# Attention with the keys on the partitions: PV in sixteen narrow matmuls, the output (not P) transposed by DMA, no row maximum, MLP last

## The chip, the cores and the metric

One core of one Trainium2 chip. The metric is the device time of one execution in microseconds (us), the median of several runs. "TensorE" is PE in the profile, "VectorE" DVE, "ScalarE" ACT. PSUM is the memory that matmuls write to, in banks; to *evict* a bank is to copy its content out, or to add it to an accumulator. PV is the product of the softmax's output P with V.

## The reference, cut to what matters

A block with adaptive layer norms: attention, then an MLP with ReLU, both on a sequence of 2048 rows of 512. Attention has 32 query heads that share 8 key/value heads of dimension 128, and looks at the last 512 keys.

```python
h = layernorm(x) * (1 + ca) + sa                 # sa, ca, ga, sb, cb, gb come from silu(c) @ w_mod
q = (h @ wq).reshape(1, 2048, 32, 128)           # wq 512 x 4096
p = softmax(q @ k.T * 128**-0.5)                 # k, v: the last W = 512 cached rows
x = x + ga * ((p @ v).reshape(1, 2048, 4096) @ wo)
h = layernorm(x) * (1 + cb) + sb
x = x + gb * (relu(h @ w1) @ w2)                 # w1 512 x 1792, w2 1792 x 512
```

## The kernel before

The rows are cut into 4 blocks of 512; a *unit* is one block and one head, 128 units in all. The loop takes one *step* per unit and records operations for each engine: `kb.op(stream, fn, reads, writes)` appends to that engine's own queue and works out the semaphores to wait for. So the order of the calls is the order in each engine's queue.

```python
def rec_qk(i, tl):          # scores, query rows on partitions: one 128x512 tile
    matmul(ps[sbk], lhsT=qT[:, 128 rows], rhs=kT[:, g, :])
    DVE  tensor_reduce(nm, ps[sbk], max, negate=True)                      # L865
    ACT  activation(P, ps[sbk], Exp, bias=nm, accum_out=lsum)              # L867

def rec_rn(i):              # normalise P, then transpose it
    DVE  reciprocal(rinv, lsum)
    POOL tensor_scalar(P, P, rinv, mult)       # x4                        # L885
    dma_start_transpose(PT, P)                 # 512 KB

def rec_pv(i, kc):          # 4 matmuls of 512 columns, V stationary       # L899
    matmul(ps[ob], lhsT=v[:, g, kc, :], rhs=PT[:, kc, :], start=(kc == 0), stop=(kc == 3))
    if kc == 3: DVE tensor_copy(oT[slot], ps[ob])                          # L914

# [...] output projection, one group of 16 matmuls per 128 rows, one PSUM bank
        def f(h, tl, t, ii):
            matmul(ps[wb], lhsT=oT[slot][:, rows], rhs=wo_sb[:, h, :], start=(ii == 0), stop=(ii == HQ - 1))  # L931
            if ii == HQ - 1:
                DVE tensor_copy / tensor_tensor(acc, ps[wb], acc, add)     # eviction, L936 / L938
            return ii == HQ - 1

def pop_wo(n, paced=False):             # one projection matmul per call ...
    if paced:
        if wo_state["skip"] > 0:        # ... but after a group has ended, one call is skipped,
            wo_state["skip"] -= 1       # so that the bank can be evicted; made up for later
            wo_state["debt"] += n
            return
        # [...]
```

The eviction is recorded in the same call as the group's last matmul. MLP matmuls (L1036, L1060) follow attention; the last projections overlap with them.

## Time and profile before

| | before |
|---|---|
| time, median | 628.3 us (627.1 to 632.0) |
| span of the profiled run | 626.4 us |
| first Q matmul | 17.8 us |
| attention, per unit | 3.67 us |
| last matmul to the end | 3.5 us |

The head of the page, with each engine's busy time:

```profile
span 626.4 us, 8650 instructions
PE 570.4 (91%) x2668; PEld 245.1 (39%) x2721; DVE 507.0 (81%) x1036; ACT 459.5 (73%) x1211; POOL 418.0 (67%) x607
```

From the list of costliest groups (line, engine, operation, output<-input, shapes, count | busy us, mean ns | idle before):

```profile
L885 POOL TENSOR_SCALAR arena<-arena 128x512 bf16<-128x512 bf16 x512 | 344.9, 692 | 88.9 <-DVE arena L878 88.5
L867 ACT ACTIVATE arena<-ps,arena 128x512 bf16<-128x512 f32 x512 | 348.0, 687 | 52.1 <-DVE arena L865 47.8
L865 DVE TENSOR_REDUCE arena<-ps 128x1 f32<-128x512 f32 x512 | 336.4, 680 | 18.1 <-PE ps L863 15.4
L899 PE MATMUL ps<-arena 128*128 128x512 bf16 x498 | 188.8, 380 | 8.8 <-DMA arena<-arena 8.4
...
L914 DVE CAST arena<-ps 128x512 bf16<-128x512 f32 x128 | 87.0, 680 | 9.5 <-PE ps L899 9.5
```

A matmul's record of 380 ns is not what it costs. In the timeline of TensorE (start, duration, what) the starts show it:

```profile
202.16 0.38 PE L899 MATMUL ps<-arena 128*128 128x512 bf16 x1
202.37 0.38 PE L931 MATMUL ps<-arena 128*128 128x512 bf16 x1
202.59 0.38 PE L863 MATMUL ps<-arena 128*128 128x512 bf16 x1
...
558.03 0.61 PE L592 MATMUL ps<-arena 128*128 128x128 bf16 x8
```

Matmuls of 512 columns start 0.2157 us apart. The last line is 8 transposes of 128 columns, each with its own weight load: 0.61 us less one record of 0.219 us, over 7, is 56 ns from start to start.

So a unit's 16 matmuls (4 each for Q, scores, PV, projection) need 3.45 us, 128 units 442 us, and the MLP's 448 need 97 us: 538 of the 626 us. TensorE bounds the kernel; the other 88 us are the start, the end, and waits in attention. In mid-attention VectorE is 97% busy. The waits (engine and line <- releaser: us in total, times, longest):

```profile
PEld ps L863 <- ACT arena L867: 69.2, 133, 1.2
PE ps L863 <- ACT arena L867: 15.8, 40, 0.7
PEld ps L931 <- DVE arena L936: 3.0, 5, 1.1
PEld ps L931 <- DVE arena L938: 2.5, 3, 0.8
```

Scores wait for the exp to free their bank. The projection hardly waits for its eviction.

### The profile page before, as it was taken

The page shows a single profiled execution, that of the slowest core. Times are in us where ns is not written, and L with a number is a line of the kernel's source. Part 1 is how long each engine was busy: PE and PEld are TensorE (multiplying, and loading weights), DVE is VectorE, ACT ScalarE, POOL GpSimd, SP SyncE. Part 2 cuts the span into 40 slices and gives each one's busy share as a digit, 9 for nine tenths or more (in the row PEclk, how much of TensorE's full clock was granted, in tenths as well). Part 3 has the DMA queues.
Part 4 walks back from the last instruction along what each step waited for, and adds up shares of the span by engine and source line. Part 5 has one row for each costly group of instructions (what it writes and reads, how often), then busy time and mean ns, then how long its engine had stood idle before and what let it go on. Part 6 is the DMA issues. An engine that isn't in the chain of part 4 may idle for free.

```text
span 626.4 us, 8650 instructions
## 1 busy us (share of the span) xinstructions
PE 570.4 (91%) x2668; PEld 245.1 (39%) x2721; DVE 507.0 (81%) x1036; ACT 459.5 (73%) x1211; POOL 418.0 (67%) x607
## 2 busy tenths in 40 slices
PE   2788789999899999999999999999989889989997
PEld 2222224344343344444434444434434334434443
DVE  4799899999899999999999999999999722362223
ACT  1799989799897888999989799989779633304310
POOL 3477769677797896778989867889969701702000
PEclk9999999999999999999999999999999989999999
DMA  9999998999997678787876878977787980000001
GB/s 234 207 225 198 219 210 155 200 211 215 196 219 134 123 123 153 142 154 149 152 146 115 159 130 148 159 137 135 135 135 131 184 224 1 1 33 1 33 26 42
DMA packets 292749, 89.17 MB, mean 142 GB/s; under 512 B 276064, under 2 KB 291680, under 8 KB 292704
## 3 DMA queue, kind: packets, MB, share of 16 engines
q1 hardware_dynamic: 292704, 88.63, 72.0%
q8 instruction: 21, 0.34, 0.2%
q14 instruction: 24, 0.20, 0.1%
HBM read 18.35 MB, written 2.10 MB: 33 GB/s over the span
## 4 chain that ended last, share of the span: by engine, by line
PE 52%; DVE 22%; DMA 11%; POOL 7%; ACT 6%; issue 2%; SPq 0%
DVE arena L865 12%; PE ps L931 11%; DMA arena<-arena 9%; PE ps L899 9%; PE ps L863 9%; PE ps L838 8%; PE ps L1060 8%; PE ps L1036 7%; ACT arena L867 5%; POOL arena L885 4%; DVE arena L599 3%; DVE arena L914 3%; DVE arena L562 2%; DMA arena<-in_B_w_dram 1%; ACT arena L847 1%
## 5 line engine op out<-in xcount | busy, mean ns | idle before, releaser
L885 POOL TENSOR_SCALAR arena<-arena 128x512 bf16<-128x512 bf16 x512 | 344.9, 692 | 88.9 <-DVE arena L878 88.5
L867 ACT ACTIVATE arena<-ps,arena 128x512 bf16<-128x512 f32 x512 | 348.0, 687 | 52.1 <-DVE arena L865 47.8
L865 DVE TENSOR_REDUCE arena<-ps 128x1 f32<-128x512 f32 x512 | 336.4, 680 | 18.1 <-PE ps L863 15.4
L863 PE MATMUL ps<-arena 128*128 128x512 bf16 x498 | 190.1, 382 | 18.9 <-ACT arena L867 15.8
L899 PE MATMUL ps<-arena 128*128 128x512 bf16 x498 | 188.8, 380 | 8.8 <-DMA arena<-arena 8.4
L838 PE MATMUL ps<-arena 128*128 128x512 bf16 x503 | 189.6, 379 | 2.2 <-DVE arena L599 0.8
L931 PE MATMUL ps<-arena 128*128 128x512 bf16 x504 | 177.4, 380 | 2.7 <-DVE arena L938 1.0
L867 ACT ACTIVATION_READ_ACCUMULATOR arena<-ps,arena 128x1 f32 x512 | 102.4, 200 | 0.0
L914 DVE CAST arena<-ps 128x512 bf16<-128x512 f32 x128 | 87.0, 680 | 9.5 <-PE ps L899 9.5
L863 PEld LDWEIGHTS ps<-arena 128*128 128x128 bf16 x512 | 49.6, 97 | 113.1 <-ACT arena L867 69.2
L847 ACT ACTIVATE arena<-ps 128x512 bf16<-128x512 f32 x128 | 76.0, 594 | 16.1 <-PE ps L838 16.1
L1049 ACT ACTIVATE arena<-ps 128x512 bf16<-128x512 f32 x56 | 33.4, 597 | 69.6 <-PE ps L1036 69.6
L899 PEld LDWEIGHTS ps<-arena 128*128 128x128 bf16 x512 | 50.1, 98 | 76.5 <-DMA arena<-arena 14.8
L931 PEld LDWEIGHTS ps<-arena 128*128 128x128 bf16 x512 | 49.6, 98 | 62.7 <-DVE arena L936 3.0
L838 PEld LDWEIGHTS ps<-arena 128*128 128x128 bf16 x512 | 50.1, 98 | 45.0 <-issue 0.8
L1036 PE MATMUL ps<-arena 128*128 128x512 bf16 x220 | 52.8, 384 | 6.5 <-DVE arena L599 2.8
L599 DVE TENSOR_SCALAR arena<-ps,arena 128x128 bf16<-128x128 bf16 x128 | 34.5, 333 | 24.0 <-PE ps L592 23.6
L1060 PE MATMUL ps<-arena 128*128 128x512 bf16 x220 | 48.8, 379 | 0.2
L1065 DVE TENSOR_TENSOR arena<-ps,arena 128x512 bf16<-128x512 f32 x16 | 11.1, 691 | 39.8 <-PE ps L1060 39.8
L943 POOL TENSOR_TENSOR arena<-arena 128x512 f32<-128x512 f32 x16 | 20.3, 1267 | 32.4 <-DVE arena L938 31.0
L1036 PEld LDWEIGHTS ps<-arena 128*128 128x128 bf16 x224 | 21.6, 98 | 32.5 <-DMA arena<-in_B_w_dram 4.4
L1060 PEld LDWEIGHTS ps<-arena 128*128 128x128 bf16 x224 | 21.8, 98 | 26.0
(40 smaller groups left out, 174.6 us busy)
## 6 DMA issues: line engine op xcount, KB each, us to landing
arena<-in_A_wq_dram SPq DMA_DIRECT2D x8, 512.0 KB, 5.4
arena<-in_A_wo_dram SPq DMA_DIRECT2D x8, 512.0 KB, 4.9
arena<-in_w_mod_dram SPq DMA_DIRECT2D x6, 512.0 KB, 5.6
arena<-in_A_x_dram SPq DMA_DIRECT2D x4, 512.0 KB, 5.3
arena<-arena SPq DMA_TRANSPOSE x128, 4.3
out_dram<-arena SPq DMA_DIRECT2D x16, 128.0 KB, 1.8
arena<-in_B_w_dram SPq DMA_DIRECT2D x1, 1792.0 KB, 8.0
arena<-in_B_w_dram SPq DMA_DIRECT2D x1, 1280.0 KB, 7.4
```

The source lines that it names most:

```text
L599: kb.op(DVE, lambda e, cc=cc: e.tensor_scalar(hnT[:, cc, ht * P:(ht + 1) * P], psb[bk][:, cc * P:(cc + 1) * P], sc_f(cc), sh_f(cc), op0=AL ...
L838: kb.op(PE, lambda e: e.matmul(ps[qb][:, :QB], wq_sb[:, k, h * Dh:(h + 1) * Dh], hnT[:, k, hn_cols(b)], start=(k == 0), stop=(k == DC - 1) ...
L847: kb.op(ACT, lambda e: e.activation(qT[qs], ps[qb][:, :QB], ACTF.Copy, scale=scale), reads=[R_ps[qb]], writes=[R_qT[qs]])
L863: kb.op(PE, lambda e: e.matmul(ps[sbk][:, :W], qT[qs][:, tl * P:(tl + 1) * P], kT_sb[:, g, :], start=True, stop=True), reads=[R_qT[qs], R_ ...
L865: kb.op(DVE, lambda e: e.tensor_reduce(nm[:, si:si + 1], ps[sbk][:, :W], axis=AX.X, op=ALU.max, negate=True), reads=[R_ps[sbk]], writes=[R ...
L867: kb.op(ACT, lambda e: e.activation(Pv[:, :, tl, :], ps[sbk][:, :W].rearrange("p (k q) -> p k q", k=KC), ACTF.Exp, bias=nm[:, si:si + 1], ...
L885: kb.op(POOL, lambda e, tl=tl, si=si: e.tensor_scalar(Pv[:, :, tl, :], Pv[:, :, tl, :], rinv[:, si:si + 1], 0.0, op0=ALU.mult, op1=ALU.add ...
L899: kb.op(PE, lambda e: e.matmul(ps[ob][:, :QB], v_sb[:, g, kc, :], PTv[:, kc, :], start=(kc == 0), stop=(kc == KC - 1)), reads=[R_v[g][kc], ...
L914: kb.op(DVE, lambda e: e.tensor_copy(oT[os_], ps[ob][:, :QB]), reads=[R_ps[ob]], writes=[R_oT[os_]], pre=pre)
L931: kb.op(PE, lambda e: e.matmul(ps[wb][:, :D], oT[slot][:, tl * P:(tl + 1) * P], wo_sb[:, h, :], start=(ii == 0), stop=(ii == HQ - 1)), rea ...
L1036: kb.op(PE, lambda e, cc=cc: e.matmul(ps[bk][:, :QB], w1_v[:, cc, fc * P:(fc + 1) * P], hnT[:, cc, hn_cols(b)], start=(cc == 0), stop=(cc ...
L1060: kb.op(PE, lambda e, fc=fc: e.matmul(ps[bk][:, :D], h1T[hb][:, fc, tl * P:(tl + 1) * P], w2_v[:, fc, :], start=(fc == 0), stop=(fc == FC ...
```

## The change

The intent: take the row maximum, the accumulator read and the normalising of P off three engines. Scores are computed transposed, keys on the partitions, so exp's output is already what PV needs. V gets a column of ones, so PV also yields the softmax sum; the normalising multiply happens on the small output, and that, not P, is transposed by DMA. Without a row maximum exp could overflow, so the sums and V are checked into a flag, and the old program stands behind a branch as the general path. The diff, cut to its core (`pv_mms(s - 1)` precedes `pop_bg(4)` in each step):

```diff
+    def s_mms(u, pr):                       # scores, keys on partitions, two tiles per exp
+        for i in range(2):
+            kc = pr * 2 + i
+            mm(s_ps[pr][:, i, :], kT_sb[:, g, kc * P:(kc + 1) * P], qT[u % NQT][:, :], True, True, ...)
+        kb.op(ACT, lambda e: e.activation(PT[u % NPT][:, pr * 2:pr * 2 + 2, :], s_ps[pr][:, :, :], ACTF.Exp, scale=scale), ...)
+
+    def pv_mms(u):                          # 16 matmuls of 129 columns, P stationary
+        for qt in range(TPB):
+            for kc in range(KC):
+                mm(o_ps[:, qt, 0:P + 1], PT[u % NPT][:, kc, qt * P:(qt + 1) * P], v_sb[:, g, kc, 0:P + 1], kc == 0, kc == KC - 1, ...)
+        kb.op(DVE, lambda e: e.reciprocal(rinv[:, u, :], o_ps[:, :, P]), ...)
+        kb.op(DVE, lambda e: e.tensor_tensor(o_sb[u % NOS][:, :, :], o_ps[:, :, 0:P], rinv[:, u, :].unsqueeze(2).to_broadcast([P, TPB, P]), op=ALU.mult), ...)
+        dma(oT[u % NOT][:, :, :], o_sb[u % NOS][...], ..., transpose=True)
+    # [...]
+    def pop_bg(n):
+        while bgq and n > 0:
+            if bgq.popleft()() != "free":
+                n -= 1
+        while bgq and getattr(bgq[0], "free", False):     # nothing has this attribute
+            bgq.popleft()()
+    # [...]
+    def enqueue_wo(b, j):                   # groups of 8 projection matmuls, one PSUM bank
+        for tl in range(TPB):
+            for i in range(HQ):
+                bgq.append(lambda ...: mm(bank[WBK], oT[slot][:, tl, :], wo_sb[:, h, :], i == 0, i == HQ - 1, ...))
+            def fin(tl=tl, t=t):            # eviction on VectorE
+                if j == 0: kb.op(DVE, lambda e: e.tensor_copy(acc[:, tl, :], bank[WBK]), ...)
+                else:      kb.op(DVE, lambda e: e.tensor_tensor(acc[:, tl, :], bank[WBK], acc[:, tl, :], op=ALU.add), ...)
+                # [...]
+                return "free"
+            bgq.append(fin)
+    # [...]
+    for s in range(NU):
+        # [...]
+        s_mms(s, 0)
+        if s + 1 < NU:
+            q_mms(s + 1)
+        s_mms(s, 1)
+        if s >= 1:
+            pv_mms(s - 1)
+        pop_bg(4)
+    # [...] MLP, the checks into the flag; then on every engine:
+                v = e.value_load(flag[0:1, 0:1])
+                with e.If(v != 128):        # [...] the general program, which is the kernel before
```

## The prediction

> **What bounds the kernel now.** TensorE. Back to back, 128x512 matmuls start 0.2157 us apart (timeline; the record of 0.38 us includes pipeline fill). Each of the 128 (block, head) units needs 16: 4 Q, 4 scores, 4 PV, 4 output projection = 3.45 us. The MLP needs 448, 97 us. That is 538 of the 626 us span. The other 88 us: 18 before the first Q matmul, 3.4 after the last matmul, the rest in the attention phase, where a unit takes 3.67 us (109 score tiles per 100 us by windows). There VectorE is 97% busy (row max 0.68 us x4, cast 0.68 us per unit), scores wait for ScalarE's exp (85 us of TensorE and weight-load waits), and in the first 100 us the DMA engines are full.
>
> **What the change removes.** The row maxes (336 us of VectorE), the 512 normalising POOL ops (345 us), the accumulator reads (102 us of ScalarE), three quarters of the transposed bytes (DMA share 0.77 in mid-attention). ScalarE keeps two exps of 1024 columns and one copy per unit: from the issue spacing of 0.52 us for a 512 copy I estimate 2.4 us. VectorE: reciprocal, multiply, half a projection eviction, about 1.3 us. DMA no longer limits. The start should shrink from 18 to about 15 us.
>
> **What it adds.** PV turns from 4 matmuls of 512 columns into 16 of 129, each with its own weight load. Here 8 transposes of 128 columns, each with its own weight load, start 56 ns apart on the warm clock, so 16 take 0.90 us against 0.86. (The Trainium skill, "TensorE: Matmul & The Clock Gate", section "Back-to-back issue gap", gives about 81 ns sustained for N=128; the trace shows 56 in bursts of 8, and I take that.) TensorE per unit: 3.49 us, practically unchanged.
>
> **A new wait.** The projection has one PSUM bank, groups of 8 matmuls, 4 per step. A finished group's eviction is not recorded with its last matmul: the loop stops at its count of 4, and the eviction is recorded in the next step, after that step's reciprocal and multiply. VectorE works in order, so every second step TensorE, having ended PV, waits for drain 0.22 + reciprocal 0.18 + multiply 0.61 + eviction 0.69 + handovers 0.1 = 1.75 us. Once the modulation rows have shifted the count by one, one matmul fits in between: 1.53 us. (The old kernel skips a slot after each group; its waits on that eviction total under 10 us.) About 58 groups end in the loop: 90 us, all on the critical path.
>
> **Sum.** Start 15; 9 steps without projection 25; 119 steps x 3.49 = 415; bubbles 90; modulation 3; remaining projection and PV 11; MLP 97; tail with flag check and branch 5: 661 us. The gain (about 60 us of old waits and start) is more than eaten by the bubbles. Without them: about 570.
>
> **What would show it.** TensorE idle before projection matmuls, released by a VectorE eviction, about 58 times 1.5 us, the largest wait of the kernel; two steps take 8.5 us, not 7.0; PV starts 56 ns apart; VectorE near 45% busy, POOL nearly idle, ScalarE about 60%; DMA share far below 0.77; PEclk 1.0 as gaps stay short; MLP still 97 us.
>
> **What would make it wrong.** If the eviction gets ahead of the multiply after all, 570 us. If weight loads limit PV to 81 ns, up to 50 us more. If the bubbles overlap other waits (exp late, transposes late), they count for less or more. A slow branch past the general code adds some microseconds.
>
> Faster 0.1, same 0.08, slower 0.82; 658 us, range 628 to 690.

## The result, and the profile after

674.8 us (673.9 to 675.5) against 628.3 us: ratio 1.0735, 95% interval 1.0689 to 1.0781, slower.

| | before | after |
|---|---|---|
| time, median | 628.3 | 674.8 us |
| first Q matmul | 17.8 | 16.6 us |
| two steps in mid-attention | 7.3 | 8.55 us |
| last matmul to the end | 3.5 | 7.9 us |
| idle of TensorE before projection matmuls, for the eviction | 1.9 | 83.0 us |

The head of the page, and the groups that answer to those of before:

```profile
span 673.8 us, 9729 instructions
PE 567.3 (84%) x4157; PEld 316.0 (47%) x4157; DVE 240.5 (36%) x531; ACT 347.6 (52%) x445; POOL 38.2 (6%) x40
...
L1456 ACT ACTIVATE PT<-psS 128x1024 bf16<-128x1024 f32 x256 | 262.8, 1027 | 225.7 <-PE psS L1350 225.6
L1350 PE MATMUL psW<-wo,oT 128*128 128x512 bf16 x512 | 139.3, 380 | 82.9 <-DVE acc L1489 58.3
...
L1466 DVE RECIPROCAL rinv<-psO 128x4 f32<-128x4 f32 x128 | 23.4, 183 | 335.8 <-PE psO L1350 335.8
...
L1350 PE MATMUL psO<-v,PT 128*128 128x129 bf16 x2048 | 137.6, 221 | 0.0
...
L1467 DVE TENSOR_TENSOR o<-psO,rinv 128x512 bf16<-128x512 f32 x128 | 88.5, 692 | 4.5
```

The intent came true: VectorE, ScalarE and POOL have all lost work, and TensorE still has about the same. But TensorE's share fell from 91 to 84%: the critical engine idles, and the second group line says where. (All matmuls have line L1350, a helper; they are told apart by tile: psW is the projection's bank.) Two steps of TensorE:

```profile
303.00 1.07 PE L1350 MATMUL psO<-v,PT 128*128 128x129 bf16 x16
303.91 1.03 PE L1350 MATMUL psW<-wo,oT 128*128 128x512 bf16 x4
...
306.50 1.07 PE L1350 MATMUL psO<-v,PT 128*128 128x129 bf16 x16
307.41 0.38 PE L1350 MATMUL psW<-wo,oT 128*128 128x512 bf16 x1
309.17 0.82 PE L1350 MATMUL psW<-wo,oT 128*128 128x512 bf16 x3 [1.39 <-DVE acc L1489]
```

and VectorE in the same stretch:

```profile
307.61 0.18 DVE L1466 RECIPROCAL rinv<-psO 128x4 f32<-128x4 f32 x1 [2.59 <-PE psO L1350]
307.83 0.69 DVE L1467 TENSOR_TENSOR o<-psO,rinv 128x512 bf16<-128x512 f32 x1
308.44 0.68 DVE L1489 TENSOR_TENSOR acc<-psW,acc 128x512 f32<-128x512 f32 x1
```

Read together: 16 PV matmuls take 0.91 us (303.00 to 303.91), 57 ns each. In the second step PV is followed by the last matmul of a projection group at 307.41. The group's eviction (L1489) waits in VectorE's queue behind the reciprocal and the multiply of the PV that has just ended, and starts at 308.44. TensorE's next matmul, the first of the next group, needs that bank and starts at 309.17. In between TensorE has nothing it may run. VectorE is idle for 2.59 us before all this. The waits of the whole kernel:

```profile
PEld psW L1350 <- DVE acc L1489: 73.1, 45, 1.8
PE psW L1350 <- DVE acc L1489: 59.9, 43, 1.6
...
PEld psW L1350 <- DVE acc L1487: 25.9, 15, 1.8
PE psW L1350 <- DVE acc L1487: 23.1, 16, 1.7
```

L1487 is the eviction of the first group of a block (a copy), L1489 that of the others (an add). 59 waits of TensorE, 59.9 + 23.1 = 83.0 us. A matmul's record is 0.38 us long where the next one can start after 0.216 us, so a wait costs about 0.16 us more than the idle time before its record shows. From the starts, two steps with a wait take 8.55 us (300.62 to 309.17) against 2 x 3.49 = 6.98 us of matmuls: 1.57 us each. Before the modulation matmuls (those of `silu(c) @ w_mod` that the loop queues at step 20), where no projection matmul stands between PV and the wait, two steps take 8.77 us: 1.79 us each. Of the 58 waits that I counted from the loop, 8 are of the long kind: 8 x 1.79 + 50 x 1.57 = 93 us.

### The profile page after: what moved, and what is told of

Read it like the earlier page. It is cut to its first block, busy times and chain, and to the rows that moved or that the text cites. A ratio compares the mean times of both kernels' runs of the same rounds, so it can differ in the third digit from the quotient of the medians.

```text
span 673.8 us, 9729 instructions
## 1 busy us (share of the span) xinstructions
PE 567.3 (84%) x4157; PEld 316.0 (47%) x4157; DVE 240.5 (36%) x531; ACT 347.6 (52%) x445; POOL 38.2 (6%) x40
## 4 chain that ended last, share of the span: by engine, by line
PE 83%; DVE 13%; issue 2%; DMA 1%; ACT 0%; ACTq 0%
PE psS L1350 24%; PE psO L1350 22%; PE psQ L1350 19%; PE psW L1350 17%; DVE o L1467 5%; DVE acc L1489 4%; DVE rinv L1466 2%; DVE acc L1487 2%; DMA wmw<-in_w_mod_dram 1%; PE psS L1353 0%; ACT qT L1448 0%; ACT PT L1456 0%; ACTq L1296 0%; DVE PT L1620 0%; DVE PT L1621 0%
## 5 line engine op out<-in xcount | busy, mean ns | idle before, releaser
L1456 ACT ACTIVATE PT<-psS 128x1024 bf16<-128x1024 f32 x256 | 262.8, 1027 | 225.7 <-PE psS L1350 225.6
L1350 PE MATMUL psW<-wo,oT 128*128 128x512 bf16 x512 | 139.3, 380 | 82.9 <-DVE acc L1489 58.3
L1350 PE MATMUL psS<-qT,kT 128*128 128x512 bf16 x512 | 153.1, 381 | 1.1 <-ACT qT L1448 1.1
L1350 PEld LDWEIGHTS psO<-v,PT 128*128 128x128 bf16 x2048 | 127.3, 98 | 30.5 <-issue 0.6
L1350 PE MATMUL psO<-v,PT 128*128 128x129 bf16 x2048 | 137.6, 221 | 0.0
L1350 PE MATMUL psQ<-hT,wq 128*128 128x512 bf16 x512 | 132.4, 381 | 0.7 <-DVE hT L1397 0.7
L1350 PEld LDWEIGHTS psW<-wo,oT 128*128 128x128 bf16 x512 | 42.6, 98 | 128.7 <-DVE acc L1489 71.4
L1467 DVE TENSOR_TENSOR o<-psO,rinv 128x512 bf16<-128x512 f32 x128 | 88.5, 692 | 4.5
L1350 PEld LDWEIGHTS psQ<-hT,wq 128*128 128x128 bf16 x512 | 50.3, 98 | 62.0 <-issue 2.0
L1350 PEld LDWEIGHTS psS<-qT,kT 128*128 128x128 bf16 x512 | 49.8, 98 | 60.5 <-issue 1.9
L1448 ACT ACTIVATE qT<-psQ 128x512 bf16<-128x512 f32 x128 | 75.7, 592 | 1.2 <-PE psQ L1350 1.2
L1489 DVE TENSOR_TENSOR acc<-psW,acc 128x512 f32<-128x512 f32 x48 | 32.7, 682 | 9.1 <-PE psW L1350 9.1
L1350 PE MATMUL psO<-wmw,wq 128*128 128x512 bf16 x140 | 31.2, 379 | 0.0
L1492 POOL TENSOR_TENSOR acc<-acc,gaf 128x512 f32<-128x512 f32 x12 | 15.2, 1268 | 257.1 <-DVE acc L1489 257.1
L1350 PE MATMUL psS<-h2T,wmw 128*128 128x512 bf16 x112 | 25.5, 379 | 0.0
L1350 PE MATMUL psS<-hT,wmw 128*128 128x512 bf16 x112 | 24.5, 379 | 0.0
L1350 PEld LDWEIGHTS psO<-wmw,wq 128*128 128x128 bf16 x140 | 13.7, 98 | 16.6
```

What stands on the lines that cost most here:

```text
L1350: kb.op(PE, lambda e: e.matmul(out_ap, lhsT, rhs, start=start, stop=stop), reads=reads, group_writes=[R_b[k] for k in bk], signal=signal)
L1448: kb.op(ACT, lambda e: e.activation(qT[u % NQT][:, :], bank[QBK], ACTF.Copy), reads=[R_b[QBK]], writes=[R_qT[u % NQT]])
L1456: kb.op(ACT, lambda e: e.activation(PT[u % NPT][:, pr * 2:pr * 2 + 2, :], s_ps[pr][:, :, :], ACTF.Exp, scale=scale), reads=[R_b[pr * 2], R ...
L1467: kb.op(DVE, lambda e: e.tensor_tensor(o_sb[u % NOS][:, :, :], o_ps[:, :, 0:P], rinv[:, u, :].unsqueeze(2).to_broadcast([P, TPB, P]), op=A ...
L1489: kb.op(DVE, lambda e: e.tensor_tensor(acc[:, tl, :], bank[WBK], acc[:, tl, :], op=ALU.add), reads=[R_b[WBK], R_acc[tl]], writes=[R_acc[tl]])
L1492: kb.op(eng, lambda e: e.tensor_tensor(acc[:, tl, :], acc[:, tl, :], gaf[:, :], op=ALU.mult), reads=[R_acc[tl], R_ga], writes=[R_acc[tl]])
```

## The experiments

Theory A: the loss is the place of the eviction in VectorE's queue, behind operations that wait for PV, together with the single projection bank. Rival B: with a single bank each reuse costs drain and eviction, whatever the order. Rival C: the narrow PV matmuls with their weight loads, or the late DMA transposes of the output, hold TensorE. The first four runs shared one chip (old kernel 628.2 us), the next four another (628.7), the next two a third (630.1), and the last had the old kernel at 630.2.

### 1. The eviction recorded at once, groups aligned to steps

```diff
+            fin.free = True
             bgq.append(fin)        # and the same for the evictions of the modulation matmuls
...
-            if bgq.popleft()() != "free":
-                n -= 1
+            r = bgq.popleft()()
+            if r != "free":
+                n -= 4 if r == "step" else 1
...
-        bgq.append(lambda: [f() for f in fs] and None)
+        bgq.append(lambda: [f() for f in fs] and "step")
```

> Edit: the eviction of a finished projection group is recorded together with the group's last matmul, and the modulation matmuls take whole steps, so that a group always ends at the end of a step. Same instructions, only the order in VectorE's queue (and the place of a few modulation matmuls) differs. Theory A (the eviction stands in VectorE's queue behind a reciprocal and a multiply that wait for the PV just ended): about 8 bubbles of 1.79 us and 50 of 1.57 us go, 93 us, and perhaps the 3 us of low clock at the modulation: 579 us, range 570 to 590; waits of TensorE for the eviction under 5 us in total; a step takes 3.5 us. Rival B (one projection bank: each reuse costs drain and eviction, about 1 us, whatever the order): about 640 us. Rival C (the narrow PV matmuls or the late DMA transposes of the output hold the projection): about 670 us.

576.5 us, correct, ratio 0.918 to the old kernel (0.915 to 0.921). The same 9729 instructions, 98 us less than the changed kernel:

```profile
span 574.8 us, 9729 instructions
PE 554.7 (97%) x4157; PEld 317.6 (55%) x4157; DVE 243.2 (42%) x531; ACT 347.5 (60%) x445; POOL 38.2 (7%) x40
...
PEld psW L1350 <- DVE acc L1492: 2.5, 4, 1.3
PE psW L1350 <- DVE acc L1492: 0.8, 1, 0.8
```

Of the waits for the eviction (now L1492) one of 0.8 us is left. A group's last four matmuls, its eviction and the first matmuls of the next group, in the same run:

```profile
303.60 1.03 PE L1350 MATMUL psW<-wo,oT 128*128 128x512 bf16 x4
304.66 0.69 DVE L1490 COPY acc<-psW 128x512 f32<-128x512 f32 x1
307.09 1.03 PE L1350 MATMUL psW<-wo,oT 128*128 128x512 bf16 x4
```

The bank is free at 305.35, 1.7 us before it is needed. B and C expected 640 and 670 us; both fall as causes of the loss. This version beats both kernels.

### 2. The eviction recorded at once, groups not aligned

Only the first part of the edit above, the lines that set `free`, for all evictions; without the `"step"`. The modulation matmuls then shift the count by one, so that a later group ends after the first of a step's four projection matmuls, and the next one begins at once.

> Edit: eviction recorded with the group's last matmul, but the count of 4 stays shifted by one after the modulation matmuls, so that from step 26 on a group ends after the first of a step's four projection matmuls and the next group starts in the same step. Theory A: the eviction is still behind that step's reciprocal and multiply, so only the 8 or so groups before the modulation profit: 674.8 - 14 = 660 us, range 655 to 666, with about 50 bubbles of 1.4 us of idle left. Rival B: about 640. If recording the eviction one step late were harmful in itself: about 580 us.

655.8 us, ratio 1.045. TensorE waits 51 times for the eviction instead of 59. Recording early does not help as long as the next group follows in the same step: VectorE still has PV's two operations ahead. Of the 19 us gained, 8 waits of 1.79 us are 14; another 3.4 us are TensorE's clock, which in the changed kernel was halved for 6.8 us after the modulation matmuls and here was not.

### 3. Groups aligned, the eviction still one step late

Only the `"step"` part of the edit of run 1.

> Edit: only the modulation matmuls take whole steps; the eviction is recorded one step late as in the changed kernel. Theory A: no projection matmul stands between PV and the wait any more, so the 50 later bubbles grow from 1.57 to 1.79 us: 674.8 + 11 = 686 us, range 680 to 690, slower than the changed kernel. Rivals B and C: 675 us, no change.

685.2 us, ratio 1.090: slower than the changed kernel by 10 us, as the lost matmul between PV and the wait asks (50 x 0.22 = 11). The half of the edit that helps in run 1 hurts alone. Runs 1 to 3 have the same matmuls; only order differs.

### 4. The old form of PV, the eviction still late (wrong result)

```diff
-        for qt in range(TPB):
-            for kc in range(KC):
-                mm(o_ps[:, qt, 0:P + 1], PT[...qt...], v_sb[:, g, kc, 0:P + 1], ...)
-        kb.op(DVE, ... reciprocal ...)
-        kb.op(DVE, ... multiply ...)
-        dma(oT[u % NOT], o_sb[u % NOS], transpose=True)
+        bk = 5 + u % 2
+        for kc in range(KC):
+            mm(bank[bk], v_sb[:, g, kc, 0:P], PT[u % NPT][:, kc, :], kc == 0, kc == KC - 1, ...)
+        kb.op(DVE, lambda e: e.tensor_copy(oT[u % NOT][...], bank[bk]), ...)
```

(`rinv` is set to 1 at the start, so that the flag stays good.)

> Edit (wrong result on purpose, softmax is not normalised): PV as in the old kernel, 4 matmuls of 512 columns per unit with V stationary; the output comes out transposed and is copied by one VectorE operation; no ones column, no reciprocal, no DMA transpose of the output. The late eviction stays. Theory A: the bubble stays, shorter by the reciprocal (0.22 us): 58 x 0.22 = 13 us, and PV is 0.045 us x 128 = 6 us shorter: 655 us, range 647 to 662, with about 58 waits for the eviction. Rival C (narrow matmuls, weight loads or late transposes are the cost): 580 us.

653.7 us, ratio 1.041; relative error 0.61, as meant. Without narrow matmuls, without reciprocal, without output transposes, the kernel is still slower than the old one, and 59 waits for the eviction remain:

```profile
PE psW L1350 <- DVE acc L1484: 50.7, 43, 1.4
PE psW L1350 <- DVE acc L1482: 19.6, 16, 1.4
```

Rival C falls by this run as well.

### 5. The version of run 1 again, as a yardstick

> The version with the eviction recorded at once and groups aligned to steps, again, as the yardstick for the next three on the same chip: 576.5 us, ratio to the old kernel 0.918.

576.5 us, ratio 0.917 (0.915 to 0.920), correct.

### 6. The same without the branch and the general program

```diff
-                v = e.value_load(flag[0:1, 0:1])
-                with e.If(v != 128):
-                    for k, n in ends:
-                        e.wait_ge(sems[k], n)
-                    gkb.emit(general[name], e)
```

(The general program is not built; the checks and the flag stay.)

> Edit: the aligned version without the read of the flag, the branch and the general program behind it (the checks on VectorE and the flag itself stay). In the changed kernel 7.9 us pass from the last matmul record to the end, in the old one 3.4 us; the output's landing and one operation in float32 account for about 1 us of the difference, so the branch is worth about 3.5 us: 573 us, range 571.5 to 575. If the branch is free: 576.5.

572.4 us, ratio 0.910 (0.908 to 0.913): the branch costs 4.1 us here. The Trainium skill says that a taken branch to a target outside the current pages forces a fetch before execution can go on ("Runtime: NRT & Kernel Launch", section "Instruction fetch mechanics"). The run shows the size of the whole, flag read included, and does not split it; the traces agree, with 3.7 us from the last matmul to the end here and 7.4 us in run 5. This version has no protection against overflow, so it is a measurement and not a proposal.

### 7. The old form of PV in the version of run 1 (wrong result)

The edit of run 4 on top of run 1.

> Edit (wrong result on purpose, not normalised): the aligned version with the old PV of 4 matmuls of 512 columns, no reciprocal, no DMA transpose of the output. This is what the narrow form costs when nothing waits. If weight loads hide and each narrow matmul takes 56 ns: 16 x 56 - 4 x 215.7 = 36 to 48 ns a unit, 5 to 6 us in all: 570.5 us, range 568 to 573.[...]

570.4 us, ratio 0.907. The narrow form with its reciprocals and transposes costs 576.5 - 570.4 = 6.1 us in all, 48 ns a unit, which is about what 0.91 - 0.863 us gives. So the weight loads cost no more than that.

### 8. The multiply twice, in the version of run 1

```diff
         kb.op(DVE, ... tensor_tensor(o_sb, o_ps, rinv, op=ALU.mult) ...)
+        kb.op(DVE, ... the same once more ...)
```

> Edit: the aligned version with the normalising multiply done twice (same values, right result): 78 us more VectorE work, total about 320 us. The eviction then ends about 2.5 us after PV, before the next projection matmul at 3.5 us: no cost, 577 us, range 575 to 580. If VectorE work as such were what the change pays for: 577 + 35 or more.

582.9 us, ratio 0.927, correct. Expected was no cost; measured is 6.4 us. VectorE has 85 us more to do (328 instead of 243), so 92% of it is hidden, but not all, and the profile names the rest:

```profile
PEld psO L1350 <- DVE o L1472: 10.6, 13, 2.0
PE psO L1350 <- DVE o L1472: 4.1, 4, 1.5
```

The first line counts weight loads; PV itself (second line) waited in 4 steps, 4.1 us, for the second multiply of the unit before (L1472) to free the output's banks. Each time VectorE had stood still for 2.2 to 3.0 us just before, at an operation of a layer norm that waited for its DMA transpose, with reciprocal and multiplies queued behind it. In run 5 VectorE has such waits too, and PV never waits for them. So this is the same lesson once more, with another operation at the head of the queue; my sum had looked at the projection bank only. Another 0.7 us is the one wait for an eviction left in run 1, which grew from 0.8 to 1.5 us; about 1 us stays unassigned.

### 9. The multiply twice, in the changed kernel

The same edit, with the late eviction.

> Edit: the changed kernel as it is (late eviction, shifted groups) with the normalising multiply done twice (right result). Theory A: each of the 58 bubbles grows by one multiply, about 0.6 us: 674.8 + 35 = 710 us, range 702 to 718; the waits for the eviction grow by the same. Rival B (bank reuse costs the same whatever stands ahead of the eviction): 675 us.

774.2 us, ratio 1.230. Much more than the 710 expected. The wait itself grew a little more than the 0.6 us expected, from 1.39 to 2.11 us, that is 58 x 0.72 = 42 us (in total from 83.0 to 125.1 us). The rest is the clock: a mean granted clock of 0.924 over a span of 770 us is (1 - 0.924) x 770 = 59 us lost, against (1 - 0.992) x 674 = 5 us in the changed kernel. The timeline shows it from a wait on:

```profile
311.86 0.38 PE L1350 MATMUL psW<-wo,oT 128*128 128x512 bf16 x1
314.35 1.46 PE L1350 MATMUL psW<-wo,oT 128*128 128x512 bf16 x3 [2.11 <-DVE acc L1491]
315.61 1.06 PE L1350 MATMUL psS<-qT,kT 128*128 128x512 bf16 x2
...
325.30 0.82 PE L1350 MATMUL psW<-wo,oT 128*128 128x512 bf16 x3 [2.11 <-DVE acc L1491]
```

The three matmuls after the first wait start 0.42 us apart (314.35 to 315.61 over 3), half the rate. After the next wait, as long as the first, they run at the full rate (0.82 us for three): not every wait halves the clock. The windows of the same run (us, then busy us and count per engine, granted clock, DMA share, GB/s), first, and those of the changed kernel:

```profile
200.00:300.00 100.00, 78.89 (x545) 42.42 (x545) 47.60 (x100) 48.24 (x60) 9.29 (x8) 0.91 0.22 42
```

```profile
200.00:300.00 100.00, 84.00 (x664) 48.51 (x662) 39.28 (x94) 57.57 (x72) 2.55 (x3) 1.00 0.37 83
```

42 + (59 - 5) = 96, and 674.8 + 96 = 771 us, against 774.2 (771.8 in the profiled run): the sum closes within 3 us.

### 10. Two projection banks, the eviction still late (wrong result)

On top of run 4: PV keeps one bank, which frees one for the projection.

```diff
-        bk = 5 + u % 2
+        bk = 5
...
+            wb = 6 + tl % 2        # and bank[wb], R_b[wb] in place of bank[WBK] in the group and its eviction
```

> Edit to the run with the wide PV (wrong result on purpose): PV keeps one bank, and the projection groups alternate between two. The eviction is still recorded one step late and still stands behind the copy of PV's output. Theory A: a group no longer needs the bank that waits for eviction, so the bubbles go although the order is the bad one: 653.7 - 58 x 1.35 = 575 us, range 567 to 585. If the late order cost TensorE time in another way than through the bank: 640 us or more.

574.6 us, ratio 0.912: 79 us less than run 4 (on another chip). The order is as bad as before, but the next group no longer needs the bank in question, and of the waits for the eviction one is left:

```profile
PE psW L1350 <- DVE acc L1485: 1.4, 1, 1.4
```

So it takes both, the late place in the queue (run 1 removes it) and the single bank (this run removes it).

### 11. Run 9 with the wait filled by useless matmuls

```diff
+                if in_loop[0]:
+                    for i in range(30):
+                        mm(bank[0][:, :P], ident[:, :], ident[:, :], True, True, [R_ident], [0], i == 29)
                 return "free"
```

> Edit to the run with the late eviction and the doubled multiply (774 us, mean granted clock 0.924): after each late eviction is recorded, TensorE gets 30 matmuls of 128 columns into a score bank that is overwritten next, 1.7 us of useless work in a wait of 2.1 us. Right result. If the excess over the expected 710 us is TensorE's clock halved in some stretches because of the longer waits (1 - 0.924 of 770 us is 59 us), the clock returns to 0.99 or more and the time falls to 674.8 + 58 x 0.72 = 716 us, range 708 to 723, although TensorE executes more. If the excess is the doubled multiply itself or another wait: 774 us or more.

722.1 us, ratio 1.145, correct, mean granted clock 0.990. With more instructions TensorE is 52 us faster than in run 9: the excess there was the clock. About 7 us of lost clock are left ((1 - 0.990) x 720).

## Why the prediction was right

- **TensorE bounds both kernels, and PV in narrow form costs next to nothing.** Right. Predicted 0.90 us for 16 matmuls; the trace shows 0.91, and run 7 shows 6.1 us in all. The Trainium skill's 81 ns for sustained N=128 ("TensorE: Matmul & The Clock Gate", section "Back-to-back issue gap") would, as an estimate ((81 - 57) ns x 2048), have asked for about 50 us more; the measurement decides, and it is 57 ns.
- **The eviction behind reciprocal and multiply stalls TensorE every second step.** Right, in place, number and size: 1.75 and 1.53 us predicted, 1.79 and 1.57 measured. (The prediction's terms, as written, add up to 1.80, not 1.75; the slip is 3 us over 58 waits.) Run 1 removes it without changing one instruction and gains 98 us: 93 of waits and 3.4 of clock, with 2 not assigned. Runs 2 and 3 show that both halves, when the eviction is recorded and where the next group starts, are needed; run 10 that a second bank does the same. The same page ("TensorE: Matmul & The Clock Gate", the table at its head) has VectorE's queue as strictly first in, first out; the timeline agrees: the eviction, whose matmul had ended, started only after the multiply.
- **Without the waits about 570.** 576.5 measured (runs 1 and 5). So the change itself gains 52 us over the old kernel (628.3 to 576.5), and the order took 98 away.
- **VectorE 45, ScalarE 60% busy.** 36 and 52% measured: both were put too high, and the longer span does not explain it (45 and 60% of the predicted 661 us would be 297 and 397 us of work; 240.5 and 347.6 were measured). In run 1, a shorter span, they are 42 and 60%. The predicted time does not rest on them, since neither engine bounds the kernel. POOL 6%, as predicted nearly idle.
- **What was mis-sized.** The sum said 661 us and 674.8 came, inside the range. Term by term, by the starts of TensorE's matmuls: the tenth step, the first with projection matmuls, was to begin at 40 us and began at 41.9; of these 1.9 us the first Q matmul made 1.6 (16.6 us instead of 15). The loop from there on was put at 508 us and took 515.1: 3.4 of that because the clock halved for 6.8 us after the modulation matmuls, whose 32 one-column matmuls stand between two waits (the prediction had a clock of 1.0 throughout), and 3 because the 58 waits cost 93 us and not 90. The rest to the end of the span took 116.8 us, not 113: the branch costs 4.1 us (run 6), where 5 was put for the whole tail, which took 7.9. One more us lies between the span of the profiled run and the median time. 1.9 + 7.1 + 3.8 + 1.0 = 13.8, the whole difference to 661.
- **What goes with the halved clock.** No run was built to test it, but the clock records of the 13 kept traces sort it. In each, the granted clock changes only at points of a fixed grid, 3.413 us apart. Take each window of this grid at full clock and count the time in which the matmuls keep TensorE at work (0.2157 us for 512 columns, from each start). The 40 windows that a halved one follows have a share of at most 0.330; the 2222 that a full one follows have at least 0.347. So it is the share of work in a window, and not the length of one wait: in run 9 the wait that ends at 314.35 lies inside one window, and the equally long one that ends at 325.30 straddles two. In the kernel before, the clock was halved at 505.0, in a wait of 2.55 us for weights of the MLP, and not by a wait of 2.82 us that ended at 561.5. What decides whether the half clock stays for one window or for two (6.8 us, seen twice) stays open.

## What to carry to other kernels

Where an engine works in order, the place of an operation in its queue is part of its cost: before recording an eviction, ask which operations stand ahead of it and what those wait for, and whether the next user of the bank comes before or after them. A change that takes much work off engines that do not bound the kernel can still lose if it puts one short operation behind the wrong wait; look for the idle time of the bounding engine first, and for the one releaser that repeats. If an accumulation has only one bank, let groups end at a step's end and evict at once, or find a second bank.

## What the Trainium skill lacked or had wrong

- "TensorE: Matmul & The Clock Gate", section "Back-to-back issue gap": about 81 ns per matmul is given as the sustained rate for N=128 with weight loads. Here 2048 matmuls of 129 columns, each with its own weight load, in bursts of 16 between wider ones, took 57 ns each (0.91 us for 16), and the wide form saved only 6.1 us in 576.5.
- The same section gives 131 ns for N=512; the matmuls of this case start 215.7 ns apart at best, the value that the section calls the isolated gap. The page is not of one mind: its section "Wait — 56ns, not 53.3ns?" has 55.6 and 215.7 ns as measured back to back.
- The same page, section "Why this matters for your kernels", asks for no idle gaps above about 3 us between bursts. Here gaps of 2.11 us, one in every two steps, brought the granted clock to 0.91 and cost 52 to 59 us (runs 9 and 11). What sorted the halvings was the share of work in a window of 3.413 us, at most 0.330 before a halving and at least 0.347 otherwise. The page has a window of this length and warns of frequent short idles elsewhere, but gives no such share.
- "Runtime: NRT & Kernel Launch", section "Instruction fetch mechanics", gives no size for a taken branch past a large program: flag read and branch cost 4.1 us here (run 6).
